# Tiles one by one, rows over two queues, blocks shared anew, and zero products in two waits

## The chip, the cores and the metric

The kernel runs on one core of a Trainium2 chip. The metric is the device time of one execution in microseconds, as the median of several runs. Five engines work side by side, each with an instruction stream of its own: TensorE (PE in the profile), VectorE (DVE), ScalarE (ACT), GpSimd (POOL) and SyncE (SP), which here only issues DMAs. GpSimd and ScalarE issue DMAs too, each on its own queue.

## The reference

The input x has 2048 tokens of 1024 features in bf16. Two layers are applied twice in turn, each on a normalised input and with a residual:

```python
x = A_x
x = x + _A_ref(_layernorm(x, axis=-1), A_w_r, A_w_i)
x = x + _B_ref(_layernorm(x, axis=-1), B_w1, B_b1, B_w2)
x = x + _A_ref(_layernorm(x, axis=-1), A_w_r, A_w_i)
x = x + _B_ref(_layernorm(x, axis=-1), B_w1, B_b1, B_w2)
```

`_A_ref` is a real two-dimensional Fourier transform over tokens and features, a product with the complex filter `w_r + 1j*w_i`, and the transform back, rounded to bf16. `_B_ref` is a dense layer to 3584 features, Mish (h times the hyperbolic tangent of its softplus), and a dense layer back to 1024.

```python
X = jnp.fft.rfft2(x.astype(jnp.float32), axes=(-2, -1)) * (w_r + 1j * w_i)
y = jnp.fft.irfft2(X, s=(S, D), axes=(-2, -1)).astype(jnp.bfloat16)
```

## The kernel before

**How it is written.** One program lists the instructions of each engine in order. `op`, `group` and `dma` add an instruction, a run of products, or a DMA, and work out its semaphore waits from resources (`Res`) that are read and written. So the order on each engine is the order of the Python calls, and an instruction that waits holds everything behind it on that engine. All DMAs have line 251. Large buffers lie in one tensor, ARENA, which is therefore the name most rows of a profile show; XS holds the 16 input tiles of 128 tokens, PS the eight banks of PSUM.

**The opening** (`prologue`, lines 382 to 413; `first_scales`, 582 to 604). x is loaded twice. First as 16 tiles of 128 tokens into XS, by seven DMAs of one to four tiles from SP and one from ScalarE (tile 10); for the mean and variance of each token VectorE handles tiles 0 to 9 (`stats_dve`, L472 and L475) and ScalarE tiles 10 to 15 (`stats_act`, L453). Then again as XR, in the arrangement that the Fourier transform needs, as 32 DMAs of 128 KB ("rows"): four quarters q of eight parts h. SP issues all of quarter 0 and the even parts of the others (20 rows), GpSimd the odd parts of quarters 1 to 3 (12 rows), after it has waited for tile 15. The table FD is loaded between quarters 2 and 3. After the rows SP issues the table JT, the first two filters `w_r`, `w_i` (four DMAs), the tables FT and BT, and small constants.

The statistics of all tiles are joined (L464 to L466), turned into one scale for each token (L444, L446), and transposed by TensorE (L596).

**Stage 1 of the first layer** (`s1`, lines 621 to 649; `scaled`, 606 to 619). The layer norm is folded into the matrix of the first Fourier step: the matrix M0 is multiplied by the scales of the tokens. That gives 16 scaled blocks, 0 to 15, in MN. Block 3 is made by ScalarE in eight instructions (L611), blocks 1, 4, 6, 8, 10, 12, 14 and 15 by GpSimd, the other seven by VectorE (L617). TensorE makes product j (eight matmuls, L636) from block j and quarter j // 4 of XR, into one of three pairs of banks. Its result is copied to Y by ScalarE (L642), or by VectorE (L644) where j leaves a rest of 1 when divided by 3. Blocks 0 to 3 are put on the engines first; block j + 4 comes after the copy of product j. Stage 2 (`s2`, L736) reads the whole of Y and FD; right after its first half come the products of the first filter (L994) and its copies on VectorE (L1005).

In the second layer's stage 1 there are no scaled blocks: XR comes from the normalised tokens, the last of them (tile 11) straight from SBUF in 16 small DMAs (`xr_direct`), in two halves. While they are under way TensorE makes 38 filler products (`spin(38, 7)`, line 1722, L653) whose result nobody reads.

**The end of a spectral layer** (`layer_A`, `residual_first`, and the first loop of `layer_B`, lines 1462 to 1466). The last of eight components (g = 7) is written to DRAM and read back in another arrangement, in four quarters. Meanwhile TensorE makes four filler products and puts the residual into all eight banks (`residual_first`, L1022). Then, for each quarter u, it adds the last transform step into banks 2u and 2u + 1 (`i4`, L1033), and ScalarE copies the banks out (`out_first`, L575). Statistics on VectorE follow, then transposes (L1143) and the first dense products (L1182).

Of the kernel before, what the change touches and what calls it, by code (L numbers as in the profile page):

```python
# [7 lines left out]
P = 128  # L8
# [172 lines left out]
class KB:  # L181
# [185 lines left out]
    def layout(self):  # L367
        K = 1024
        self.o = dict(XR=0, Z=0, X=12 * K, T=20 * K, YK=28 * K, V=40 * K, JT=48 * K, M0=49 * K, IDF=49 * K + 256, RT=50 * K,
                      JUNK=51 * K, WR=54 * K, YS=96 * K, UT=64 * K, MN=64 * K, Y=96 * K, XN=128 * K, U=128 * K,  # L370
# [11 lines left out]
    def prologue(self):  # L382
        sp = self.sp
        self.op(self.pool, lambda e: e.memset(self.EPS[:], 1e-5), writes=[self.r_eps, self.r_warm])
        xt = self.x[0].rearrange("(t p) d -> p t d", p=P)

        for a, b in ((10, 11), (0, 1), (1, 3), (11, 12), (3, 6), (12, 14), (6, 10), (14, 16)):
            self.dma(self.act if a == 10 else sp, self.XS[:, a:b, :], xt[:, a:b, :], f"x{a}", writes=self.r_xs[a:b])
        self.warm(ACT.Sqrt)
        small = {}  # L390
        def load_small(name, n, d):
            b = self.alloc(name, self.o[name], [n], d)
            self.dma(sp, b.ap, self.con[name], name.lower(), writes=[b.res])
            small[name] = b
        load_small("M0", P, BF)
        load_small("IDF", P, F32)
        self.M0, self.IDF = small["M0"], small["IDF"]

        self.XR = self.alloc("XR", self.o["XR"], [P, P])
        self.r_xr = []  # L400
        xv = self.x[0].rearrange("(n2 n1) (h l) -> h n2 n1 l", n2=16, l=P)
        for q in range(4):
            r = Res(f"xr{q}")
            for h in range(8):
                prog = self.pool if q and h % 2 else sp
                self.dma(prog, self.XR.ap[h:P:8, 32 * q:32 * q + 32, :], xv[h][:, 32 * q:32 * q + 32, :], f"xr{q}{prog.name}",
                         parts=[r], reads=[self.r_xs[15]] if prog is self.pool else [])
            self.r_xr.append(r)
            if q == 2:
                self.dma(sp, self.FD[:], self.con["FD"], "fd", writes=[self.r_fd])  # L410
        load_small("JT", 4 * P, BF)
        self.JT, self.r_jt = small["JT"].ap, small["JT"].res
        self.w1_next = 0
# [192 lines left out]
    def scaled(self, j):  # L606
        rt = self.RT
        rc = rt.ap.rearrange("p a b -> p (a b)")
        if j == 3:
            for n in range(8 * j, 8 * j + 8):  # L610
                self.op(self.act, lambda e, n=n: e.activation(self.MN.ap[:, n, :], self.M0.ap, ACT.Copy, scale=rc[:, n:n + 1]),  # L611
                        reads=[rt.res, self.M0.res], parts=[self.r_mn[j]])
            return

        n = slice(8 * j, 8 * j + 8)
        prog, sc, res = (self.pool, rc, rt.res) if j in (1, 4, 6, 8, 10, 12, 14, 15) else (self.dve, self.PS[:, 7, 0:P], self.r_bank[7])
        self.op(prog, lambda e: e.tensor_tensor(self.MN.ap[:, n, :], self.M0.ap.unsqueeze(1).to_broadcast([P, 8, P]),  # L617
                                                sc[:, n].unsqueeze(2).to_broadcast([P, 8, P]), ALU.mult),
                reads=[res, self.M0.res], parts=[self.r_mn[j]])

    def s1(self, li):
        self.Y = self.alloc("Y", self.o["Y"], [P, P])
        self.Y.res.begin()
        M, XR = self.M, self.XR
        for j in range(4 if not li else 0):
            self.scaled(j)
        for j in range(16):
            if not li and self.npair % 4 == 3:

                self.npair += 1  # L630
            ps, banks, _ = self.pair()
            fns = []
            for q in range(8):
                n = 8 * j + q
                m = M[:] if li else self.MN.ap[:, n, :]
                fns.append(lambda e, q=q, n=n, ps=ps, m=m: e.matmul(ps[:, q * P:(q + 1) * P], XR.ap[:, n, :], m,  # L636
                                                                   start=True, stop=True))
            self.group(fns, reads=[self.r_xr[j // 4], self.r_m if li else self.r_mn[j]], writes=banks)
            src = ps.rearrange("p (q k) -> p k q", q=8)
            dst = self.Y.ap[:, :, 8 * j:8 * j + 8]  # L640
            if (j % 2 or j == 8) if li else j % 3 != 1:
                self.op(self.act, lambda e, dst=dst, src=src: e.activation(dst, src, ACT.Copy), reads=banks, parts=[self.Y.res])  # L642
            else:
                self.op(self.dve, lambda e, dst=dst, src=src: e.tensor_copy(dst, src), reads=banks, parts=[self.Y.res])  # L644
            if not li and j + 4 < 16:
                self.scaled(j + 4)
        for r in ([self.MN.res, self.M0.res] + self.r_xr if not li else []):
            r.r(self.pe, self.pe.count)
            self.XR.res.r(self.pe, self.pe.count)

    def spin(self, n, bank):

        self.group([lambda e: e.matmul(self.PS[:, bank, :], self.BD[:, 0:P], self.BD[:, 0:512], start=True, stop=True)] * n,  # L653
                   reads=[self.r_bd], writes=[self.r_bank[bank]])

    def ring(self, name, n, size, shape):
        return [self.alloc(f"{name}{i}", self.o[name] + size * i, shape) for i in range(n)]
# [48 lines left out]
    def layer_A(self, li):  # L706
# [6 lines left out]
        o, K = self.o, 1024  # L713
        dve, act, sp, pool = self.dve, self.act, self.sp, self.pool
        ring, load_tabs, load_btabs, load_w = self.ring, self.load_tabs, self.load_btabs, self.load_w
        WT, FT, BT = self.WT, self.FTr, self.BTr
        FD, BD = self.FD, self.BD
# [7 lines left out]
        def zslot(g, i):  # L725
            return Z[(2 * g + i) % 6]

        def s2(g, half):
# [14 lines left out]
            else:  # L743
# [16 lines left out]

            zz = self.ARENA[:, o["Z"] // 2 + (2 * g % 6) * K:o["Z"] // 2 + (2 * g % 6 + 2) * K].rearrange(
                "p (s r k) -> p s r k", s=2, r=2)
# [157 lines left out]
        self.s1(li)  # L920
        if li:
            self.rest_of_filter()
        Z = ring("Z", 6, 2 * K, [2, 512])
        X = ring("X", 4, 2 * K, [2, 512])
        T = ring("T", 4, 2 * K, [2, 512])
# [32 lines left out]
                u_turn(g, h)  # L958
        self.spin(4, 0)
        self.residual_first()  # L960
        if li == 0:
            self.op(self.pool, lambda e: e.tensor_copy(self.B1[:], self.B1h[:]), reads=[self.r_b1h], writes=[self.r_b1])
        self.w1_buf = [self.alloc(f"W1_{i}", (self.ob["WS"] + i * 4096, 140 * K)[i > 4], [8, 256]) for i in range(4 if li else 6)]
# [155 lines left out]
    def layer_B(self, li, last):  # L1119
        pe, dve, act, sp, pool = self.pe, self.dve, self.act, self.sp, self.pool  # L1120
# [208 lines left out]
        def products(p, s_off, stages, extra, loads=True):  # L1329
# [14 lines left out]
            def s_sum(dst, x, y, op, k):  # L1344
                f = slice(7 * k, 7 * k + 7)
                self.op(dve, lambda e: e.tensor_tensor(ap[dst][:, f, :], ap[x][:, f, :], ap[y][:, f, :], op),  # L1346
                        reads=part(x, k) + part(y, k), writes=part(dst, k))
            s3, s1, s2, s4 = (lambda k, a=a: s_sum(*a, k) for a in (
                ("S", "A11", "A21", ALU.subtract), ("A21", "A21", "A22", ALU.add), ("A11", "A21", "A11", ALU.subtract),
                ("S", "A12", "A11", ALU.subtract)))  # L1350
# [53 lines left out]
            if stages is STD:  # L1404
                sums = {(0, 3): [(s1, 0)], (2, 0): [(s1, 1)], (2, 2): [(s2, 0)], (3, 0): [(s2, 1)], (3, 2): [(s4, 0)], (4, 1): [(s4, 1)]}
            else:
                sums = {(0, 1): [(s1, 0)], (0, 3): [(s1, 1)], (1, 1): [(s2, 0)], (1, 3): [(s2, 1)], (2, 3): [(s4, 0)], (3, 1): [(s4, 1)]}
# [53 lines left out]

        for u in range(4):
            self.i4(0, 4, 32 * u, 32, 2 * u)
            self.out_first(u, 0, act)
            for j in range(2):
                self.stats_quarter(j, u)
# [252 lines left out]
                self.xr_load(10)  # L1719
        products(1, self.ob["XT2"], stages, extra)  # L1720
        if not last:
            self.spin(38, 7)


def build_kernel(nc, A_x, A_w_r, A_w_i, B_x, B_w1, B_b1, B_w2, out):
# [35 lines left out]
```

## Time and profile before

| What | Value |
|---|---|
| Time, median of 3 runs | 933.21 us (932.65 to 934.0) |
| Time of the profiled execution | 934.83 us |
| Its span in the profile | 933.0 us |
| TensorE busy | 870.8 us, 93% of the span |
| VectorE, ScalarE, GpSimd busy | 620.8, 434.8, 158.9 us |
| Opening: first product of stage 1 / first of stage 2 | 24.23 / 40.60 us |
| First layer: last component written / first `i4` product | 106.81 / 116.17 us |
| Second layer: first filler product / first stage 1 product | 480.27 / 488.47 us |
| Second layer: last component written / first `i4` product | 558.67 / 566.33 us |

The profile is of one execution; times in it count from the start of the span. A name such as L636 is a line of the kernel. A busy TensorE is not one at its peak, as its matmuls are pipelined and their ends modelled. The idle time of an engine only matters where the chain of work that ended last passes through it.

The page's row on the granted TensorE clock, in 40 slices of 23.3 us, reads 9 (90% or more of full speed) in all but two slices, those from 117 us (8) and from 560 us (7).

### The profile page before, as it was taken

The page shows a single profiled execution, that of the slowest core. Times are in us where ns is not written, and L with a number is a line of the kernel's source. Part 1 is how long each engine was busy: PE and PEld are TensorE (multiplying, and loading weights), DVE is VectorE, ACT ScalarE, POOL GpSimd, SP SyncE. Part 2 cuts the span into 40 slices and gives each one's busy share as a digit, 9 for nine tenths or more (in the row PEclk, how much of TensorE's full clock was granted, in tenths as well). Part 3 has the DMA queues.
Part 4 walks back from the last instruction along what each step waited for, and adds up shares of the span by engine and source line. Part 5 has one row for each costly group of instructions (what it writes and reads, how often), then busy time and mean ns, then how long its engine had stood idle before and what let it go on. Part 6 is the DMA issues. An engine that isn't in the chain of part 4 may idle for free.

```text
span 933.0 us, 13477 instructions
## 1 busy us (share of the span) xinstructions
PE 870.8 (93%) x5404; PEld 470.5 (50%) x5479; DVE 620.8 (67%) x985; ACT 434.8 (47%) x641; POOL 158.9 (17%) x183
## 2 busy tenths in 40 slices
PE   0699689999999999999998987999999999999998
PEld 0577477444444444444447766764444444444443
DVE  6698367677698767558856865666747665554473
ACT  6798476455313385520009975847650015552000
POOL 3923002970003652010121200000000000000000
PEclk9999989999999999999999997999999999999999
DMA  9969862683886488364732795444166635732432
GB/s 277 256 232 294 220 162 67 223 301 102 294 246 222 154 301 321 132 207 156 275 103 79 236 224 145 159 152 165 57 192 191 198 126 194 278 119 76 175 123 111
DMA packets 147679, 175.99 MB, mean 189 GB/s; under 512 B 68872, under 2 KB 126312, under 8 KB 147496
## 3 DMA queue, kind: packets, MB, share of 16 engines
q1 hardware_dynamic: 134848, 128.81, 45.3%
q0 software_dynamic: 10672, 44.67, 13.2%
q10 hardware_dynamic: 2096, 1.64, 0.6%
q8 instruction: 43, 0.70, 0.3%
q14 instruction: 20, 0.16, 0.1%
HBM read 130.78 MB, written 40.89 MB: 184 GB/s over the span
## 4 chain that ended last, share of the span: by engine, by line
PE 84%; DVE 4%; ACT 4%; SPq 4%; DMA 3%; issue 1%; POOL 0%; ACTq 0%; DVEq 0%
PE PS L1321 36%; PE PS L1222 29%; PE PS L1182 6%; SPq L251 4%; PE PS L810 2%; PE PS L736 2%; PE PS L1033 2%; PE PS L835 2%; PE PS L1143 1%; DMA ARENA<-c_bt 1%; DMA ARENA<-u_scratch 1%; PE PS L653 1%; DMA u_scratch<-ARENA 1%; ACT ARENA L453 1%; DVE ARENA L792 1%
## 5 line engine op out<-in xcount | busy, mean ns | idle before, releaser
L1321 PE MATMUL PS<-ARENA 128*128 128x512 bf16 x1535 | 338.2, 379 | 1.7
L1222 PE MATMUL PS<-ARENA 128*128 128x512 f16 (+1 forms) x1265 | 279.0, 379 | 2.0 <-DVE ARENA L1227 0.8
L1321 PEld LDWEIGHTS PS<-ARENA 128*128 128x128 bf16 x1568 | 153.4, 98 | 184.4
L1227 DVE TENSOR_TENSOR ARENA<-PS,ARENA 128x512 f32<-128x512 f32 x230 | 157.1, 691 | 100.0 <-PE PS L1222 92.1
L1222 PEld LDWEIGHTS PS<-ARENA 128*128 128x128 bf16 x1288 | 125.4, 98 | 153.2 <-DVE ARENA L1227 3.5
L1232 ACT ACTIVATE ARENA<-ARENA,B 128x512 bf16<-128x512 f32 x138 | 98.8, 720 | 69.1 <-DVE ARENA L1227 63.7
L575 ACT ACTIVATE ARENA<-PS 128x512 f32<-128x512 f32 (+2 forms) x84 | 61.9, 742 | 115.1 <-PE PS L1222 92.3
L1115 POOL TENSOR_TENSOR ARENA<-ARENA 128x512 bf16<-128x512 bf16 x56 | 71.4, 1274 | 75.0 <-DVE ARENA L524 61.3
L453 ACT ACTIVATE ARENA<-XS 128x1024 bf16<-128x1024 bf16 x60 | 63.2, 1053 | 38.0 <-DVE XS L1372 33.1
L1182 PE MATMUL PS<-ARENA 128*128 128x256 bf16 (+1 forms) x524 | 74.1, 297 | 1.7 <-ACT ARENA L1186 1.4
L1346 DVE TENSOR_TENSOR ARENA<-ARENA 128x3584 bf16<-128x3584 bf16 x32 | 63.9, 2016 | 0.0
L1372 DVE TENSOR_TENSOR XS<-PS,ARENA 128x512 bf16<-128x512 f32 x52 | 35.7, 689 | 39.1 <-PE PS L1321 38.7
L1182 PEld LDWEIGHTS PS<-ARENA 128*128 128x128 bf16 x528 | 50.9, 99 | 20.5 <-ACT ARENA L1186 2.5
L1364 DVE TENSOR_TENSOR ARENA<-PS,ARENA 128x512 f32<-128x512 f32 x48 | 32.9, 688 | 28.1 <-PE PS L1321 27.7
L1186 ACT ACTIVATE ARENA<-PS,B 128x256 bf16<-128x256 f32 (+1 forms) x66 | 33.3, 516 | 29.6 <-PE PS L1182 29.3
L1232 ACT ACTIVATE ARENA<-PS,B 128x512 bf16<-128x512 f32 x46 | 31.5, 685 | 18.4 <-PE PS L1222 18.4
L1360 DVE TENSOR_TENSOR ARENA<-ARENA,XS 128x512 f32<-128x512 f32 x52 | 36.9, 734 | 0.6
L810 PE MATMUL PS<-ARENA 128*128 128x256 bf16 x256 | 32.4, 273 | 4.2 <-DVE ARENA L799 3.2
L444 ACT ACTIVATE RS<-MV,EPS 128x1 f32<-128x1 f32 (+2 forms) x11 | 3.3, 296 | 70.8 <-DVE MV L566 70.1
L788 ACT ACTIVATE ARENA<-PS 128x1024 bf16<-128x1024 f32 x32 | 33.3, 1071 | 4.5 <-PE PS L784 4.5
L792 DVE TENSOR_TENSOR ARENA<-ARENA 128x1024 bf16<-128x1024 bf16 x32 | 22.0, 688 | 19.5 <-ACT ARENA L788 13.8
L736 PE MATMUL PS<-FD,ARENA 128*128 128x256 bf16 (+1 forms) x256 | 31.8, 271 | 2.5 <-ACT ARENA L642 1.3
(97 smaller groups left out, 814.1 us busy)
## 6 DMA issues: line engine op xcount, KB each, us to landing
ARENA<-in_B_w_dram SPq DMA_DIRECT2D x30, 896.0 KB, 6.7
ARENA<-w1s_scratch SPq DMA_DIRECT2D x28, 896.0 KB, 4.6
ARENA<-w2s_scratch SPq DMA_DIRECT2D x24, 896.0 KB, 6.4
w1s_scratch<-ARENA POOLq DMA_DIRECT2D x14, 896.0 KB, 4.1
ARENA<-in_B_w_dram SPq DMA_DIRECT2D x24, 512.0 KB, 4.6
u_scratch<-ARENA SPq DMA_DIRECT2D x14, 512.0 KB, 3.5
ARENA<-u_scratch SPq DMA_DIRECT2D x14, 512.0 KB, 6.2
w2s_scratch<-ARENA POOLq DMA_DIRECT2D x8, 896.0 KB, 4.2
```

The source lines that it names most:

```text
L251: return eng.dma_start(out_ap, in_ap).then_inc(ds.sem, 16)
L453: self.op(act, lambda e, i=i, f=f: e.activation(junk.ap, x, f, accum_out=sums[:, i:i + 1]), reads=[self.r_xs[j]], writes=[junk.res], parts ...
L575: fn = (lambda e: e.activation(dst, src, ACT.Copy)) if scale is None else \
L736: fns.append(lambda e: e.matmul(dst, at(r), FD[:, t:t + n], start=start, stop=stop))
L810: fns.append(lambda e, c=c, part=part: e.matmul(ps[:, c * 256:(c + 1) * 256], yk.ap[:, part, c * P:(c + 1) * P], t[:, (128, 0)[part]:(384, ...
L1115: self.op(self.pool, lambda e, dst=A(dst), x=A(x), y=A(y), op=op: e.tensor_tensor(dst, x, y, op), reads=[b.res] + list(after), writes=[b.rs])
L1182: fns.append(lambda e, db=db, bank=bank, fl=fl: e.matmul(PS[:, bank, 0:w], wb.ap[:, db, fl * P:(fl + 1) * P], x.ap[:, db, tok], start=(db ...
L1222: self.group([lambda e, db=db: e.matmul(PS[:, bank, :], A[:, db, :], mov[:, db, :], start=(start and db == 0), stop=(db == 3), skip_group_ ...
L1227: self.op(dve, lambda e: e.tensor_tensor(dst.ap, PS[:, bank, :], x.ap, ALU.add), reads=[self.r_bank[bank], x.res], writes=[dst.res])
L1232: self.op(act, lambda e: e.activation(at, src, ACT.Mish, bias=self.B1[:, ft:ft + 1]), reads=[res, self.r_b1], writes=[ra])
L1321: self.group([lambda e, i=i, k=k, b=PB[n][k].ap: e.matmul(PS[:, bank, :], ap[:, i, t * P:(t + 1) * P], b[:, i - 7 * k, :], start=(start an ...
L1346: self.op(dve, lambda e: e.tensor_tensor(ap[dst][:, f, :], ap[x][:, f, :], ap[y][:, f, :], op), reads=part(x, k) + part(y, k), writes=part ...
```

## The change

It has five parts.

1. The tiles are loaded by 13 DMAs instead of 8: singly, but for 4 and 5, 6 and 7, 8 and 9. Tile 10 still comes from ScalarE.
2. GpSimd issues 19 of the 32 rows instead of 12: the odd parts of all quarters, and part 0 of quarters 1 to 3. It waits for tile 13 instead of 15. SP issues the other 13, and FD after all its rows instead of between quarters 2 and 3.
3. The scaled blocks: ScalarE makes block 1 instead of 3; GpSimd makes 2, 4, 9, 10, 11 and 13; VectorE the other nine. Of the copies of stage 1, VectorE keeps three (5, 10, 14) instead of five, and ScalarE has 13 instead of 11.
4. A new function, `hold`, makes n products of a weight matrix of zeros (ZERO, set by GpSimd after stage 1) with the constant table BD and adds them to bank 7. It is called after `residual_first`, with 16 products in the first layer and 11 in the second, and with two more between the first and the second quarter of `i4`.
5. The filler before the second layer has 33 products instead of 38.

```diff
-        for a, b in ((10, 11), (0, 1), (1, 3), (11, 12), (3, 6), (12, 14), (6, 10), (14, 16)):
+        for a, b in ((10, 11), (0, 1), (1, 2), (11, 12), (2, 3), (3, 4), (12, 13), (4, 6), (13, 14), (6, 8), (14, 15), (8, 10), (15, 16)):
             self.dma(self.act if a == 10 else sp, self.XS[:, a:b, :], xt[:, a:b, :], f"x{a}", writes=self.r_xs[a:b])
...
-                prog = self.pool if q and h % 2 else sp
+                prog = self.pool if h % 2 or q and not h else sp
                 self.dma(prog, self.XR.ap[h:P:8, 32 * q:32 * q + 32, :], xv[h][:, 32 * q:32 * q + 32, :], f"xr{q}{prog.name}",
-                         parts=[r], reads=[self.r_xs[15]] if prog is self.pool else [])
+                         parts=[r], reads=[self.r_xs[13]] if prog is self.pool else [])
             self.r_xr.append(r)
-            if q == 2:
-                self.dma(sp, self.FD[:], self.con["FD"], "fd", writes=[self.r_fd])
+        self.dma(sp, self.FD[:], self.con["FD"], "fd", writes=[self.r_fd])
...
-        if j == 3:
+        if j == 1:
             for n in range(8 * j, 8 * j + 8):
...
-        prog, sc, res = (self.pool, rc, rt.res) if j in (1, 4, 6, 8, 10, 12, 14, 15) else (self.dve, self.PS[:, 7, 0:P], self.r_bank[7])
+        prog, sc, res = (self.pool, rc, rt.res) if j in (2, 4, 9, 10, 11, 13) else (self.dve, self.PS[:, 7, 0:P], self.r_bank[7])
...
-            if (j % 2 or j == 8) if li else j % 3 != 1:
+            if (j % 2 or j == 8) if li else j not in (5, 10, 14):
...
+    def hold(self, n, bank):
+
+        self.group([lambda e: e.matmul(self.PS[:, bank, :], self.ZERO.ap, self.BD[:, 0:512], start=False, stop=False,
+                                       skip_group_check=True)] * n,
+                   reads=[self.r_bd, self.ZERO.res], writes=[self.r_bank[bank]])
...
         self.s1(li)
         if li:
             self.rest_of_filter()
+        self.ZERO = self.alloc("ZERO", o["RT"], [P])
+        self.op(pool, lambda e: e.memset(self.ZERO.ap, 0.0), writes=[self.ZERO.res])
...
         self.spin(4, 0)
         self.residual_first()
+        self.hold(11 if li else 16, 7)
...
         for u in range(4):
             self.i4(0, 4, 32 * u, 32, 2 * u)
+            if u == 0:
+                self.hold(2, 7)
             self.out_first(u, 0, act)
...
         if not last:
-            self.spin(38, 7)
+            self.spin(33, 7)
```

## The prediction

> **What bounds the kernel now.** I read the chain of work that ended last first, because it says where an earlier start is worth something, then the timeline of the opening, then the granted clock by stretches.
>
> ```profile
> PE 84%; DVE 4%; ACT 4%; SPq 4%; DMA 3%; issue 1%; POOL 0%; ACTq 0%; DVEq 0%
> ```
>
> TensorE ends the run for 84% of the span, and from 223 us to the end almost without a gap. What the change can touch lies in the other 16%: the opening (the first 41 us), the waits at the end of each spectral stage, and the filler products before the second one. Whatever they gain moves all later work, since the main loops follow in a fixed order.
>
> The opening, by the timeline (start, duration, engine, line; in brackets the wait and what ended it), first GpSimd's alone, then all engines:
>
> ```profile
> 16.11 7.61 POOL L251 DMA_DIRECT2D ARENA<-in_A_x_dram  x12 [15.25 <-DMA XS<-in_A_x_dram]
> 23.81 14.87 POOL L617 TENSOR_TENSOR ARENA<-ARENA 128x1024 bf16<-128x1024 bf16 x8
> ```
> ```profile
> 10.90 1.06 ACT L453 ACTIVATE ARENA<-XS 128x1024 bf16<-128x1024 bf16 x1 [1.40 <-DMA XS<-in_A_x_dram]
> ...
> 20.56 0.17 DVE L464 TENSOR_SCALAR MV<-BN 128x12 f32<-128x12 f32 x1 [1.03 <-ACT ARENA L453]
> ...
> 38.83 0.61 PE L636 MATMUL PS<-ARENA 128*128 128x128 bf16 x8 [0.58 <-POOL ARENA L617]
> ...
> 39.47 1.02 ACT L642 ACTIVATE ARENA<-PS 128x1024 bf16<-128x1024 f32 x1 [0.17 <-PE PS L636]
> ```
>
> The reader is to see three limits. ScalarE ends the statistics (VectorE waits 1.03 us for it), having lost 1.40 us to tiles 12 and 13, which come as one transfer. GpSimd sits until 16.11 for tile 15 before it issues its rows. And its eight scaled blocks end last: block 15 at 38.7 us, its product at 38.83, its copy at 40.49, then stage 2 at 40.60. In the same 15 to 18 us the DMA engines are a third idle (columns: stretch, length, busy of each engine, clock, DMA share, GB/s):
>
> ```profile
> 15.00:18.00 3.00, 0.00 (x0) 0.00 (x0) 2.90 (x8) 2.73 (x6) 1.89 (x3) 1.00 0.66 143
> 18.00:24.00 6.00, 0.48 (x1) 0.18 (x1) 3.82 (x12) 3.78 (x11) 5.90 (x11) 1.00 1.04 265
> ```
>
> The ends of the two spectral stages, in the same columns; first layer above, second below:
>
> ```profile
> 112.40:116.20 3.80, 0.03 (x2) 0.06 (x3) 0.00 (x0) 0.00 (x0) 0.00 (x0) 1.00 0.60 133
> 116.90:120.30 3.40, 2.81 (x106) 2.70 (x102) 2.26 (x6) 2.35 (x5) 0.00 (x0) 0.53 0.40 115
> ...
> 123.70:127.10 3.40, 3.40 (x31) 2.95 (x29) 3.26 (x7) 2.85 (x3) 0.00 (x0) 0.53 1.19 291
> ```
> ```profile
> 564.10:567.50 3.40, 1.05 (x33) 0.88 (x32) 0.00 (x0) 0.18 (x1) 0.00 (x0) 0.96 0.60 136
> 567.50:570.90 3.40, 2.65 (x96) 2.64 (x96) 1.60 (x5) 1.61 (x3) 0.00 (x0) 0.50 0.28 72
> 570.90:574.30 3.40, 1.55 (x21) 1.26 (x18) 3.20 (x10) 2.49 (x6) 0.00 (x0) 0.50 1.13 306
> 574.30:577.70 3.40, 3.40 (x35) 3.28 (x36) 2.57 (x5) 2.99 (x4) 0.00 (x0) 0.53 1.03 257
> ```
>
> TensorE stands idle while the last component goes to DRAM and back; then its clock is half for 6.8 us of the first layer and 10.2 of the second. The page's clock row dips in these two slices alone.
>
> **What the Trainium skill says.** "TensorE: Matmul & The Clock Gate", Part 1, says that the clock is gated to half after an idle window of about 3.4 us, that the window runs free of the kernel, and that a busy window releases it. The trace agrees: the half-clock stretches are multiples of 3.41 us, each after such a wait. It does not say whether products with zero weights count as activity; no line here shows it. "DMA: Bandwidth & Descriptors", Issuing engines are not separate DMA queues, says that more queues only save issue time; the 0.66 share shows a stretch where issue time is what lacks. "SBUF — State Buffer", SBUF size, gives GpSimd's descriptors 16 KiB of a partition; with 16 B each on 16 partitions ("DMA: Bandwidth & Descriptors", SWDGE vs HWDGE vs iDMA) an estimate is 16,384 places, against 19 rows x 512 pieces = 9,728, so a full ring is unlikely. No run here shows it.
>
> **The change, part by part.**
>
> *Tiles singly.* ScalarE has six tiles of about 2.37 us from 4.75, so 18.95 if it never waits, against 20.53. VectorE has ten of 1.40 from 4.57, so about 18.8 with small waits. Do tiles arrive? Two were there by 4.75, the eighth at 9.64 and the tenth at 10.90: 0.8 us a tile. In the new order ScalarE's tiles are the 4th, 7th, 10th, 13th and 16th, due 6.2, 8.6, 11.0, 13.5 and 15.9, and it needs them at 7.1, 9.5, 11.9, 14.2 and 16.6. So 1.55 us off the chain to the roots; blocks can start at 21.3 instead of 22.87. SP issues 12 instead of 7 at 0.52 us: its rows start at about 8.1, not 5.6, behind tiles that still fill the queue.
>
> *Rows.* GpSimd waits for tile 13 (the tenth, 11.0) and issues 19 rows at 0.634 us (7.61 / 12): free at 23.1, before 23.8. Queued behind this wait on GpSimd are its blocks. SP issues 13 rows instead of 20. The idle third of 15 to 18 us, 1.0 us of DMA time, fills, so rows, FD (now after the rows, first read at stage 2) and the filter loads come at least 1.0 us earlier. The last row landed at 35.9, FD takes about 2.5 us and lands by 35 us or so, under a stage 2 start at 37.
>
> *Blocks.* GpSimd has 6 x 1.86 = 11.2: ends 34.3, not 38.7. ScalarE makes block 1 (2.45) and 13 copies of 0.97: 21.45 + 2.45 + 12.6 = 36.5, plus 0.6 waiting for block 13's product: 37.1. VectorE makes 9 blocks of 1.17 and 3 copies of 1.22, 14.2 us, ending 36.7. This walk (each product waits for its block, its row quarter and a free pair of banks) gives 40.6 for the kernel before, measured 40.49. So stage 1 ends 3.4 us earlier, now bound by ScalarE. Late next is the first filter's load: it landed at 39.42, now at 38.4 if only the idle 1.0 us is gained; its product comes 0.87 us after stage 2 starts, at 38.0. It holds TensorE 0.4: I take **-3.0**. Bounds: -3.8 if the loads come 2.4 earlier, as fewer short pieces on SP's queue suggest, and the walk is a little cautious; -1.5 if only the statistics' gain comes through. The long wait at 70 to 80 us (BT's load, 9.5 us) is started by events that move along, so I carry the gain through.
>
> *Zero products, first layer.* 16 x 0.216 (the rate of the filler, L653) = 3.5 us in a wait of 3.8: they end 0.3 before the component lands. The memset is 0.1 us on an idle GpSimd. Two more between quarters cost 0.43 where the second quarter has landed, as here. Gain if the clock stays full: ahead of the first block of layer B the transposes take 1.42 (elsewhere 1.07), the fifteen small products 1.20 (0.64) and sixteen of L1182 2.48 (1.75), 1.6 on the chain, of which 1.4 follows after VectorE's copies. Net **-1.0**; bounds -1.5 and +0.8 (clock falls all the same, and the component comes early enough to be held up).
>
> *Second layer.* 11 x 0.216 = 2.4 in a wait of 2.1: 0.3 late, then 0.43, both under the second quarter, which lands at 568.2. Transposes 1.89 to 1.07, small products 1.20 to 0.64, L1182 1.90 to 1.75: 1.5. I take **-1.4**; bounds -1.7 and +0.3.
>
> *Filler 38 to 33.*
>
> ```profile
> 481.78 6.85 PE PS L653 x31
> 488.63 0.46 PE PS L636 x8
> ```
> ```profile
> ARENA<-ARENA SPq DMA_DIRECT2D x6, 16.0 KB, 2.4
> ```
>
> The chain runs through the filler (first fence), not through the rows. Of SP's six direct rows, issued from 483.34 on in 3.73 us, the third goes out at about 484.6 and takes 2.4 us (second fence: size and median time to landing): the first half lands near 487.0, and 33 products end at 487.55. The gain is 5 x 0.216 = 1.08; the second half, about 488.9, is needed after eight more groups. **-1.0**, bounds -1.1 and -0.3.
>
> Sum: -3.0 - 1.0 - 1.4 - 1.0 = **-6.4**. The profiled execution took 934.83 (span 933.0 and 1.8 around it), so it would be 928.4; it stood 1.6 above the median 933.21, so the median is **926.8**.
>
> **Rivals.**
> 1. *The clock falls all the same* (zero weights don't count, or the later gaps of 1.7 us are enough, as after 120.3). For it: the second half-speed stretch of the first layer follows a window with 1.57 us busy. Against: at 77 to 80 us TensorE is idle 3 us with a full clock after. Then -3.0 - 1.0 + 0.4 = -3.6: 929.6.
> 2. *The opening's gain is eaten by loads.* Tables and filters queue behind the same rows; stage 2 starts early and waits. For it: the chain of before passes through the filter's load (34.42, 4.99 us). Then -0.8 - 2.4 - 1.0 = -4.2: 929.0.
> 3. *Slower: GpSimd's issue.* Block 2 is now the third product and lies behind 19 issues. For it: the longest single issue in the trace is 1.09 us; 19 such end at 31.7, block 13 at 42.9, its copy and that of block 15 at about 45.6, 5.1 later than now. With the other -3.4 that is +1.7: 934.9. It decides from about 1.0 us an issue, where the opening loses 3.4. Against: twelve in a row took 0.634 each under the same statistics.
>
> **How the numbers follow.** Forecast 0.60 (own range 924.8 to 929.0), clock 0.17, loads 0.10, GpSimd 0.09, anything else 0.04. The range 924.8 to 931.8 takes in the first three with their bounds and leaves out the slower case and the tails. A difference of 0.2% is 1.9 us, about what a measurement of this kernel can tell from no change. Faster beyond it: 0.83; within: 0.08; slower: 0.09.
>
> **What would show it.** GpSimd's first row at about 11 us and its first block at 23; L464 at 19; stage 2 (L736) at 37 to 38; clock 1.00 in the 10 us after each component; the filler ending at the same distance before L636. A first block on GpSimd past 27 us, L736 after 40, or half clock after the zero products would show a step wrong; so would TensorE waiting for rows after 33 filler products.

## The result, and the profile after

The changed kernel takes 933.63 us (median of 6 runs, 932.72 to 934.68), the kernel before in the same comparison 933.43 (6 runs, 932.39 to 934.0). The ratio is 1.0004 with an interval of 0.9991 to 1.0017: no change that can be measured, where 926.8 was forecast. The profiled execution took 934.68 us with a span of 932.9 (before 934.83 and 933.0).

Following one point of each stage through the two profiles splits the forecast sum into what came of each term. A minus is earlier; each row is the change within its own stretch. The component goes to DRAM in two writes; "written" is the start of the first. In the views of the changed kernel a line has its number there: L635 is L636 of the kernel before, L1041 its L1033, L1190 its L1182.

| Term | Forecast, us | Profile, us | Read from (before, after) |
|---|---|---|---|
| Opening, carried to the last component | -3.0 | 0.0 | stage 2 at 40.60, 40.90; component written at 106.81, 106.81 |
| End of the first layer | -1.0 | +0.41 | 17th product of L1190 (before: L1182) at 128.51, 128.92 |
| Filler 38 to 33 | -1.0 | -1.07 | stage 1 of layer 2 at 488.63, 487.97, so -0.66, of which +0.41 was there before |
| End of the second layer | -1.4 | +0.50 | 17th product of L1190 at 579.67, 579.51 |
| Sum | -6.4 | -0.16 | span 933.0, 932.9 |

**The opening.** GpSimd does what was forecast. In the timeline of the changed kernel (start, duration, engine, line; in brackets the wait and what ended it) its rows begin at 10.51 us, one every 0.63 us, and its blocks at 22.55. The instruction that joins the statistics (L464 before, L463 here) begins at 19.19, against 20.56:

```profile
10.51 11.94 POOL L251 DMA_DIRECT2D ARENA<-in_A_x_dram  x19 [9.65 <-DMA XS<-in_A_x_dram]
22.55 11.16 POOL L616 TENSOR_TENSOR ARENA<-ARENA 128x1024 bf16<-128x1024 bf16 x6
```

TensorE, in the same view, makes products 0 to 3 early (8 + 24 matmuls) and then stands still:

```profile
24.12 2.74 PE L635 MATMUL PS<-ARENA 128*128 128x128 bf16 x24 [0.25 <-ACT ARENA L610]
29.45 8.03 PE L635 MATMUL PS<-ARENA 128*128 128x128 bf16 x80 [2.59 <-issue]
37.98 0.62 PE L635 MATMUL PS<-ARENA 128*128 128x128 bf16 x8 [0.51 <-DVE ARENA L616]
39.12 0.62 PE L635 MATMUL PS<-ARENA 128*128 128x128 bf16 x8 [0.51 <-DVE ARENA L616]
40.90 1.03 PE L741 MATMUL PS<-FD,ARENA 128*128 128x256 bf16 x8 [1.16 <-DVE ARENA L643]
```

Product 4 is the first that needs quarter 1 of the rows. The profile puts its 2.59 us down to "issue", that is, to nothing that it shows; the semaphore events in the trace name the row: the last one of quarter 1 on SyncE's queue, issued at 15.20 us, signals its landing at 29.36. GpSimd's rows of that quarter were all there by 22.82. The rest of the stage then runs late into VectorE, which the chain of waits shows (start, length, what): the copy of product 10, then blocks 14 and 15 queued behind it, then the last copy.

```profile
26.86 2.59 issue
29.45 6.10 PE PS L635 x56
35.55 0.02 issue
35.58 1.23 DVE ARENA L643
36.80 2.26 DVE ARENA L616 x2
39.06 1.15 DVE ARENA L643
```

The pause has a second cost. The 56 matmuls behind it take 6.10 us, 0.109 each; in the run with early quarters below, 24 take 1.51, 0.063 each. This slow stretch ends at 35.36 us, where the trace has its first record of the granted clock; before it the views print 1.00 without a record.

Why the row was late is in the DMA view of 24 to 28 us (the packets of all queues; then each queue's packets, MB and share of 16 engines), and in the view of SyncE's own DMAs from 18 to 34 us (duration of one issue, then issue to landing: least, median, most):

```profile
DMA packets 643, 0.93 MB, mean 232 GB/s; under 512 B 437, under 2 KB 437, under 8 KB 643
...
q0 software_dynamic: 305, 0.84, 91.6%
q1 hardware_dynamic: 338, 0.08, 14.3%
```
```profile
L251 SPq DMA_DIRECT2D ARENA<-in_A_x_dram x6: 630/1834/4734, 15.9 to 28.8; - x6
...
DMA to landing us min/median/max: 3.3/7.2/13.6
```

q0 is GpSimd's queue, q1 that of SyncE. 206 packets are over 2 KB (643 less 437) and carry the 0.84 MB: 4096 bytes each. SyncE's have 256 bytes (0.08 MB in 338). In these 4 us SyncE's queue moved a tenth of what GpSimd's did. Over the longer stretch its issues took from 0.63 us to as much as 4.73, and one row took 13.6 us to land. The rows of GpSimd's queue that landed in the 4 us are of quarters 2 and 3, which nothing needed yet.

**The ends of the spectral stages.** The zero products run where they were meant to, and the clock is full through the wait. It falls one window later (stretch, length, busy of TensorE, weight loads, VectorE, ScalarE, GpSimd, then clock, DMA share, GB/s); the first layer first, then the second:

```profile
117.53:120.94 3.41, 2.59 (x97) 2.45 (x95) 2.41 (x7) 2.37 (x5) 0.00 (x0) 1.00 0.79 222
120.94:124.35 3.41, 1.82 (x31) 1.67 (x32) 3.05 (x9) 3.19 (x6) 0.00 (x0) 0.96 1.19 295
124.35:127.76 3.41, 3.41 (x30) 2.83 (x28) 3.38 (x7) 2.84 (x4) 0.00 (x0) 0.54 1.15 279
```
```profile
568.10:571.50 3.40, 2.00 (x81) 1.90 (x77) 2.24 (x8) 2.55 (x5) 0.00 (x0) 0.96 0.66 187
571.50:574.90 3.40, 2.95 (x30) 2.75 (x31) 2.65 (x7) 2.60 (x5) 0.00 (x0) 0.50 1.20 290
574.90:578.30 3.40, 3.40 (x29) 2.85 (x28) 3.21 (x7) 2.76 (x4) 0.00 (x0) 0.53 0.60 144
```

Before, the first layer had two half-clock stretches of 3.4 us; now it has one, the second of them. The second layer has 6.8 us instead of 10.2. The trace's records of the clock put the two falls at 124.11 and 571.25, so each lies about a quarter of a microsecond before the end of a stretch shown here. The timeline of the first layer:

```profile
112.14 3.66 PE L657 MATMUL PS<-BD,ARENA 128*128 128x512 bf16 x16
116.34 0.95 PE L1041 MATMUL PS<-MT,ARENA 128*128 128x32 bf16 x32 [0.54 <-DMA ARENA<-u_scratch]
117.35 0.38 PE L657 MATMUL PS<-BD,ARENA 128*128 128x512 bf16 x1
117.57 2.55 PE L1041 MATMUL PS<-MT,ARENA 128*128 128x32 bf16 x96
121.78 0.81 PE L1041 MATMUL PS<-MT,ARENA 128*128 128x96 bf16 x15 [1.67 <-ACT XS L574]
123.34 1.24 PE L1151 MATMUL PS<-IDENT,ARENA 128*128 128x128 bf16 x16 [0.75 <-DVE ARENA L523]
```

After `i4` TensorE waits 1.67 us for ScalarE to copy out, and 0.75 us for VectorE before the transposes. The second pause and most of the first lie in the 3.41 us before the fall, 120.70 to 124.11, of which TensorE is busy 1.58.

**The filler** works as forecast: 6 + 26 recorded products, then stage 1 at once, on the chain, with no wait for rows.

```profile
480.85 1.29 PE PS L652 x6
482.14 0.05 issue
482.19 5.78 PE PS L652 x26
487.97 0.46 PE PS L635 x8
```

### The profile page after: what moved, and what is told of

The parts are those of the page before. It is cut to its first block, busy times and chain, and to the rows that moved or that the text cites. A ratio compares the mean times of both kernels' runs of the same rounds, so it can differ in the third digit from the quotient of the medians.

```text
span 932.9 us, 13539 instructions
## 1 busy us (share of the span) xinstructions
PE 878.9 (94%) x5428; PEld 476.0 (51%) x5505; DVE 619.2 (66%) x985; ACT 436.9 (47%) x643; POOL 160.0 (17%) x190
## 4 chain that ended last, share of the span: by engine, by line
PE 85%; ACT 5%; DVE 5%; DMA 3%; issue 1%; POOL 0%; SPq 0%; ACTq 0%; DVEq 0%
PE PS L1329 36%; PE PS L1230 29%; PE PS L1190 6%; ACT ARENA L452 2%; PE PS L815 2%; PE PS L741 2%; PE PS L1041 2%; PE PS L840 2%; PE PS L635 1%; PE PS L1151 1%; DMA ARENA<-c_bt 1%; DMA ARENA<-u_scratch 1%; DMA u_scratch<-ARENA 1%; PE PS L652 1%; DVE ARENA L797 1%
## 5 line engine op out<-in xcount | busy, mean ns | idle before, releaser
L1190 PE MATMUL PS<-ARENA 128*128 128x256 bf16 (+1 forms) x524 | 75.1, 300 | 1.7 <-ACT ARENA L1194 1.4
L1190 PEld LDWEIGHTS PS<-ARENA 128*128 128x128 bf16 x528 | 51.4, 100 | 21.0 <-ACT ARENA L1194 2.5
```

Of the source, the lines that this page charges most:

```text
L1190: fns.append(lambda e, db=db, bank=bank, fl=fl: e.matmul(PS[:, bank, 0:w], wb.ap[:, db, fl * P:(fl + 1) * P], x.ap[:, db, tok], start=(db ...
```

## The experiments

Two things had to be explained: why quarter 1 came late, and why the zero products gave nothing. All edits are against the changed kernel unless said otherwise. The kernel before was run beside each set, with medians of 932.53, 933.05 and 932.24 us, so ratios are compared rather than times. The time of one execution varies by several microseconds (the kernel before: 930.48 to 935.22 in 46 runs).

### The rows as before

```diff
-                prog = self.pool if h % 2 or q and not h else sp
+                prog = self.pool if q and h % 2 else sp
...
-                         parts=[r], reads=[self.r_xs[13]] if prog is self.pool else [])
+                         parts=[r], reads=[self.r_xs[15]] if prog is self.pool else [])
             self.r_xr.append(r)
-        self.dma(sp, self.FD[:], self.con["FD"], "fd", writes=[self.r_fd])
+            if q == 2:
+                self.dma(sp, self.FD[:], self.con["FD"], "fd", writes=[self.r_fd])
```

> The changed kernel with the rows as before: GpSimd 12 of 32 after tile 15, SP 20, FD between quarters 2 and 3. Theory (GpSimd's rows go ahead of SP's on the DMA engines, so a row of quarter 1 on SP came only when GpSimd's 19 were through): quarter 1 lands at about 27.0 and quarter 3 at 35.8 as in the kernel before, product 4 of stage 1 starts near 27 instead of 29.45, and stage 2 begins at 39.5 to 40.0 instead of 40.90. Rival (quarter 1 is late because tiles and constants of SP come first, whoever issues the rows): product 4 stays at 29 or later and stage 2 at 40.5 or later.

932.17 us, ratio 0.9995 (0.9984 to 1.0006). In its profile product 4 starts at 28.9 us and stage 2 at 40.6. So undoing the rows brings the opening back by 0.3 us only, close to the rival's side; the 27 us of the theory did not come. With 12 rows on GpSimd's queue and 20 on its own, SyncE's part of quarter 1 is there at 28.9, hardly earlier than with 19 and 13: the old division isn't the one that the earlier statistics and new blocks need.

### GpSimd takes the quarters needed first

```diff
-                prog = self.pool if h % 2 or q and not h else sp
+                prog = self.pool if q < 2 else sp
```

> The changed kernel with all 16 rows of quarters 0 and 1 on GpSimd and all of quarters 2 and 3 on SP. Theory (GpSimd's queue goes ahead): quarters 0 and 1 land by 19 and 24, SP's after that at 0.65 us a row, by 29 and 33; TensorE never waits for rows, stage 2 begins at 37.5 to 38.5, 2.5 to 3.4 us earlier than in the changed kernel. If what follows keeps it, the time is 0.25 to 0.35 percent lower; if the wait for BT's table to 79.97 takes it (it ended at the same 79.97 in both kernels although stage 2 began 0.3 apart), the last component is still written at 106.8 and the time doesn't change. Rival (the DMA engines share evenly and the total decides): quarter 1 lands at 27 or later and stage 2 begins after 40.

931.5 us, ratio 0.999 (0.9982 to 0.9998). The timeline of TensorE:

```profile
27.39 1.51 PE L635 MATMUL PS<-ARENA 128*128 128x128 bf16 x24 [0.83 <-DMA ARENA<-in_A_x_dram]
...
33.18 1.51 PE L635 MATMUL PS<-ARENA 128*128 128x128 bf16 x24 [0.69 <-DMA ARENA<-in_A_x_dram]
...
36.93 1.03 PE L741 MATMUL PS<-FD,ARENA 128*128 128x256 bf16 x8 [1.16 <-DVE ARENA L643]
38.98 0.63 PE L1002 MATMUL PS<-ARENA 128*128 128x256 bf16 x4 [1.01 <-DMA ARENA<-in_A_w_i_dram]
```

Product 4 starts at 27.39 and stage 2 at 36.93, 3.97 us before that of the changed kernel and inside the 37 to 38 of the forecast, but for 0.07. So the blocks and copies were walked rightly, and the landing of quarter 1 was what spoiled it. The filter's load now holds TensorE 1.01 us, the "late next" of the forecast. The wait for the table BT moves along (9.29 us, from 67.39), and the last component is written at 103.65, 3.16 earlier than in the changed kernel. The kernel was run again in the last set:

> The kernel of e2_gpsimd_early_quarters once more, as the partner on the same chip of the two kernels without zero products: early rows, 16 + 2 and 11 + 2 zero products, no fill. 930.5 to 932.

932.01 us, ratio 0.9998 (0.9982 to 1.0014). Stage 2 at 37.30, but the last component only at 105.42, 1.4 earlier than in the changed kernel. In this execution the filter's load held TensorE 1.11 us, and the granted clock was at half from 39.58 to 42.99. It is the exception: in the other 13 profiles of this document, the kernel before among them, the component is written 65.8 to 67.1 us after the start of stage 2, here 68.1. So a start gained in the opening is carried through, as the forecast had it, if the clock isn't lost right behind it. In the medians this edit alone is worth about 1 us, not told apart from nothing.

### No row on GpSimd at all

```diff
-                prog = self.pool if h % 2 or q and not h else sp
+                prog = sp
```

> All 32 rows on SyncE's queue, none on GpSimd's. If GpSimd's packets of 4096 bytes hold up SyncE's of 256, SyncE's rows now come at an even pace: the 16 rows of quarters 0 and 1 are there by 26 us, no row takes more than 9 us from its issue to its landing, and SyncE has no single issue over 2.5 us after the tiles. If SyncE's queue is slow of itself in this stretch (its own issuing, or the table loads beside it), quarter 1 is not there before 28 us, and issues of 3 us and more stay. In both cases the last quarter is later than in the changed kernel, 33 us or more, so the time is no better.

A single run took 934.38 us. The DMA view of 24 to 28 us and SyncE's own DMAs from 18 to 34 us, as shown above for the changed kernel:

```profile
DMA packets 3158, 0.79 MB, mean 198 GB/s; under 512 B 3157, under 2 KB 3157, under 8 KB 3157
...
q1 hardware_dynamic: 3157, 0.78, 86.8%
```
```profile
L251 SPq DMA_DIRECT2D ARENA<-in_A_x_dram x22: 627/628/636, 17.8 to 31.9; - x22
...
DMA to landing us min/median/max: 2.8/3.1/5.3
```

With GpSimd's queue empty, SyncE issues a row every 0.63 us without one exception, and a row lands 3.1 us after its issue. The same queue moved 0.78 MB in these 4 us, against 0.08. TensorE's timeline then has product 4 in one run with products 1 to 3, and pays at quarter 3, whose last row has 31 in front of it:

```profile
23.92 5.62 PE L635 MATMUL PS<-ARENA 128*128 128x128 bf16 x56 [0.25 <-ACT ARENA L610]
...
36.23 3.29 PE L635 MATMUL PS<-ARENA 128*128 128x128 bf16 x32 [3.57 <-DMA ARENA<-in_A_x_dram]
40.68 1.03 PE L741 MATMUL PS<-FD,ARENA 128*128 128x256 bf16 x8 [1.16 <-DVE ARENA L643]
```

For quarter 1 this settles where the cause lies: neither the issuing nor the bandwidth of SyncE's queue is short; it is GpSimd's queue beside it. In the changed kernel both queues together moved more (232 against 198 GB/s), but rows that were not needed first.

### The changed kernel once more

> The changed kernel itself once more, on the chip that the next kernels use. If the landing of SyncE's rows is decided anew in every execution, product 4 of stage 1 starts at another time than 29.5 us (between 26 and 31 us), and stage 2 moves with it (36.7 to 41.5), while the GpSimd queue's last row lands at 29 to 32 us as before. If the order of the instructions decides it, product 4 starts within 0.5 us of 29.5. Time against the kernel before: 0.998 to 1.001 in both cases.

934.31 us, ratio 1.0009 (0.9993 to 1.0025), 12 runs from 929.19 to 936.8. Product 4 at 29.12, stage 2 at 39.85. Two further kernels below have the same code in the opening, and there product 4 starts at 27.94 and 26.57, stage 2 at 38.76 and 36.75. The repeat alone would have spoken for a landing fixed by the order of the instructions, being within 0.4 of 29.45. With the other two it is decided anew in each execution, 26.57 to 29.45 in four profiles, and the opening that was forecast does occur, with the same code, in one of the four. The share of SyncE's queue goes with it: in the same 4 us it moved 0.21, 0.14, 0.13 and 0.08 MB where product 4 starts at 26.57, 27.94, 29.12 and 29.45.

### The zero products left out

```diff
-        self.hold(11 if li else 16, 7)
...
-            if u == 0:
-                self.hold(2, 7)
```

> The changed kernel without any zero products (16 and 2 in the first layer, 11 and 2 in the second). Theory (they keep the clock through the wait itself, but a window of 3.4 us with two short pauses right after it drops it all the same, and the two between the quarters cost 0.4 in the first layer): the clock falls in the first layer just after the component lands, and again from about 124; the second half of the first layer's end is 0.4 earlier relative to the component's landing; the time is within 0.1 percent of the changed kernel. Rival (the zero products gain what was forecast, hidden by another loss): 1.5 to 2.5 us slower than the changed kernel.

931.78 us, ratio 0.9983 (0.9969 to 0.9997), against 1.0004 (0.9991 to 1.0017) and 1.0009 (0.9993 to 1.0025) with them: faster without them by about 0.2%, which neither side of the expectation had; the intervals just overlap. Half clock at 114.5 to 121.3 and 565.0 to 571.9. To have the openings alike, the same edit was made to the kernel with the early quarters:

> The same with all zero products left out, so that the difference is theirs alone. The forecast had them at a gain of 2.0 (1.0 + 1.4 less 0.4 for the two more): then this is 2 us slower than its partner, 933. If they cost time, as the two profiles with and without them suggest (the component has landed before they end, and the clock falls after them all the same), it is 1 to 2 us faster, 929.5 to 930.5.

930.12 us (20 runs, 928.86 to 931.86), ratio 0.9976 (0.9968 to 0.9984), against 0.9998 for its partner and 0.999 for the same kernel in the first set: the zero products cost 1.3 to 2 us, where they were forecast to gain 2.4. The profiles show why they gain little: the clock falls all the same. They don't show the cost: from the write of the last component to the 17th product of L1190 they explain 0.6 us in the first layer and 0.5 in the second, and of the 2.4 us between the two spans (931.1 and 928.7) 1.6 are there when the component is written, before any zero product. Nor is it the clock: over all executions its mean is 0.995 to 0.996 with the zero products and 0.992 without them, so half clock became shorter and the time longer. What costs the rest stays open.

### The pauses after `i4` filled

```diff
         self.root(0, 2)
+        self.spin(3, 0)
         rest(0)
+        self.spin(3, 4)
```

> The changed kernel with three filler products before the first small products of the transform's rest and three more before the transposes, in free banks, so that the pauses of 1.7 and 0.7 us after the last component are shorter. Theory (the window with those pauses is what drops the clock): the clock stays full from the component to the dense layer in both layers, transposes 1.07 instead of 1.24 to 1.89 and sixteen L1182 products 1.75 instead of 2.66, 1.0 to 1.5 us for each layer, so 0.1 to 0.3 percent faster than the changed kernel. Rival (zero weights count as idle, so the wait before is what drops it): half clock as in the changed kernel, no gain.

932.31 us, ratio 0.9993 (0.9978 to 1.0009), runs from 927.93 to 936.23. Its profile, of an execution of 927.93, has full clock from the opening to 925.5 us, and the transposes take 1.08 us, the sixteen products of L1190 1.92 with nothing at half rate. The clock is measured in every execution, not only in the profiled one: its mean is 1.000 in 5 of these 12 and in none of the 18 of the changed kernel. So filling the two pauses can keep the clock, though not each time. What it is worth in time isn't resolved here, within a spread of 8 us.

### Early quarters, fill, and the number of zero products

The three edits together, with 16 and 11, with 9 and 6, with none, and with 9 and 11 zero products after `residual_first`:

```diff
-        self.hold(11 if li else 16, 7)
+        self.hold(11 if li else 9, 7)
```

> GpSimd takes all of quarters 0 and 1, SyncE quarters 2 and 3, and the pauses of the second layer's end are filled with products of no use (3 and 4 of them). If the two repairs are independent: stage 2 starts at 36.5 to 37.5 us, the clock is full from the last component to the end, and the time is 926 to 928.5, 0.993 to 0.996 of the kernel before. If the early start is given back at the last component (table BT), or the fill only moves the throttling elsewhere, it is 930 or more.

> As the kernel before it in this list, with 9 zero products instead of 16 in the first layer's wait and 6 instead of 11 in the second's. If the zero products often end after the component has landed (16 last 3.7 us, and i4 begins 7.7 us after the write at the earliest, where 6.25 us were seen without them), this gains up to 1 us more: 925 to 928. If the shorter run of products lets the clock fall before i4, it loses 1 to 2 us against it.

> Early rows and the products of no use in the pauses before the transposes, but no zero products. If the fill keeps the clock only together with the zero products, the clock falls at the first i4 of each layer and this is no faster than without the fill, 929.5 to 930.5. If the fill does it alone, 927.5 to 929.

> Early rows, fill, 9 zero products in the first layer and 11 in the second (with 6 there the clock fell at 562.4 us, with 11 it didn't). If the 6 lost what the throttle took (6.8 us at half clock, 1 to 2 us) it is faster than the kernel with 9 and 6 (0.9964): 0.994 to 0.996 of the kernel before. If the 11 end after the component has landed, that is given back, and it is 0.996 to 0.998.

| Early quarters, and | us | Ratio (interval) | Half clock at the two ends in the profile, us | Executions with a mean clock of 1.000 |
|---|---|---|---|---|
| 16 and 11, no fill | 932.01 | 0.9998 (0.9982 to 1.0014) | 3.4 and 3.4 | 0 of 12 |
| none, no fill | 930.12 | 0.9976 (0.9968 to 0.9984) | 10.2 and 6.8 | 0 of 20 |
| none, fill | 930.04 | 0.9977 (0.9965 to 0.9989) | 3.4 and 3.4 | 0 of 10 |
| 16 and 11, fill | 930.17 | 0.998 (0.9969 to 0.999) | 0 and 0 | 12 of 20 |
| 9 and 6, fill | 929.35 | 0.9964 (0.9954 to 0.9974) | 0 and 6.8 | 7 of 20 |
| 9 and 11, fill | 928.85 | 0.9961 (0.995 to 0.9973) | 0 and 0 | 6 of 11 |

The kernel with 16 and 11 missed the 926 to 928.5 that two independent repairs would give: its clock was full, but in its profile stage 2 began at 38.57 instead of 36.5 to 37.5, the filter's load held TensorE 1.4 us at 39.6, and the component was written at 105.69. The one with 9 and 6 missed its range by 1.35 us and lost the clock in the second layer, as its expectation had for too short a run. The one without zero products came out as expected where the fill needs them: half clock at the first `i4`, and no gain from the fill (930.04 against 930.12). Zero products alone lose 1.3 to 2 us, fill alone gives nothing, and only with both did an execution keep the full clock throughout, in about half of the cases. Within each of the three kernels that have both, the executions with a mean clock of 1.000 have a median 1.7 to 1.9 us below that of the others; this is what was seen, not what an edit brought about. The kernel with 9 and 6 took 0.8 us less than that with 16 and 11 on the same chip, but their intervals overlap, so the number of zero products is not shown to matter. The last kernel lies on the border of its two ranges. Its timeline in stretches of 3.41 us, with the two pauses, now filled, in the second line:

```profile
110.53:113.94 3.41, 3.29 (x104) 2.64 (x103) 0.83 (x3) 1.19 (x2) 0.00 (x0) 1.00 0.34 75
113.94:117.35 3.41, 2.23 (x54) 1.78 (x51) 3.25 (x10) 2.86 (x6) 0.00 (x0) 1.00 0.84 240
117.35:120.76 3.41, 3.12 (x44) 2.35 (x41) 3.12 (x7) 3.26 (x4) 0.00 (x0) 1.00 1.19 295
```

The clock stays full. Busy time alone does not decide that, though. In the changed kernel's second layer it fell after 3.41 us with 2.26 busy (567.84 to 571.25), more than the 2.23 here. And in the kernel with no row on GpSimd, which has 16 zero products and no fill, it stayed full in the first layer after 3.41 us with 1.76 busy (120.98 to 124.39) and both pauses. Of the twelve layer ends that were profiled with 16 or 11 zero products and no fill, this is the only one that kept the clock. The timeline of the last kernel shows the zero products end just as the component lands:

```profile
108.61 2.15 PE L657 MATMUL PS<-BD,ARENA 128*128 128x512 bf16 x9
110.88 0.95 PE L1041 MATMUL PS<-MT,ARENA 128*128 128x32 bf16 x32
...
115.98 0.82 PE L652 MATMUL PS<-BD 128*128 128x512 bf16 x3 [1.18 <-ACT XS L574]
```

That is 6.5 us after the second, last write of the component. With 16 products `i4` began 7.85 to 9.22 us after it in all eight profiles; with 9, at 6.50 and 6.53; with none, at 6.25, 6.61 and 8.36, and in the kernel before at 8.29. In the changed kernel the 16 end 7.92 us after the write, so they would hold a component that lands at 6.3 back by 1.6 us. In seven of the eight the component landed after their end, though; whether they delay the landing itself was not tried.

The kernel with 9 and 11 has the lowest median of all: 928.85 us, 0.9961 of the kernel before, and faster than the changed kernel too by the two ratios. It is not told apart from the one with 9 and 6, nor clearly from the one that has neither zero products nor fill (930.12), since the intervals overlap.

## Why the prediction was wrong

**Statistics and tiles: right.** 19.19 for the 19 that was to be looked for (L463 here, L464 before), 1.37 us earlier for the 1.55 of the forecast, ScalarE without its wait of 1.40.

**GpSimd's issue: right.** 0.628 us a row (11.94 / 19), first block at 22.55. The slower rival, stretched issues on GpSimd, did not happen. The stretch fell on SyncE. Nor did a full ring show, which the forecast had called unlikely: the 19 issues took 0.63 to 0.79 us each. (The 16 bytes of a descriptor that its estimate uses stand in the section Terms of the page it names.)

**Rows: the step that failed.** The forecast had it that the idle third "fills, so rows, FD (now after the rows, first read at stage 2) and the filter loads come at least 1.0 us earlier". That holds for the last row, which the trace has at 32.1, against 35.9, for FD at 34.4 and for the first filter, at 38.4 as forecast. It does not hold for quarter 1, the one that product 4 needs, at 29.36. The walk gave every quarter the gain of the mean. The rest of that part holds: with the same opening in the run with fill, product 4 starts at 26.57 and stage 2 at 36.75. The Trainium skill, "DMA: Bandwidth & Descriptors", Queues, rings and completion order, has what might have warned: each engine takes turns between queues packet by packet. The forecast drew on the same page only for issue time and for the room for descriptors. The trace agrees in direction: with packets of 4096 bytes beside 256, SyncE's queue moved a tenth of what GpSimd's did (0.08 and 0.84 MB); strict turns would give a sixteenth, an estimate from the two sizes. But in the kernel before, with the same sizes and in the same 4 us, SyncE's queue moved 0.33 MB beside 0.62. So the sizes alone don't set the share, and no run here separates them from another advantage of GpSimd's queue. The rival "opening's gain is eaten by loads" had -0.8 left of it; what took it were rows, not tables.

**Zero products: the second step that failed.** "Gain if the clock stays full" had a condition, and it fell. Zero weights do count: the half-clock stretch from 116.7 is gone. But the forecast took each half-clock stretch to follow the long wait ("each after such a wait"). The one from 123.5 did not: the 3.41 us ahead of it (120.10 to 123.51, busy 1.39) already held the two pauses behind `i4`, which zero products in the wait don't touch. The first rival had named them. With the zero products the clock still falls there, and with the pauses filled it can stay full. So in the first layer the part behind `i4` takes 8.80 us before and after. What is left is +0.41 ahead of it: `i4` begins 0.17 later and takes 0.24 longer with the two extra products, which were put at 0.43. In the second layer the part behind `i4` takes 9.41 instead of 8.68, since the half clock now lies over the products of L1190 (2.82 us for sixteen, 2.10 before); 0.23 of this was made up ahead of it. The skill, "TensorE: Matmul & The Clock Gate", HAM oscillation — how this bites in real kernels, gives the rule of no idle gap over about 3.4 us. Here no gap was longer than 1.67, and the clock fell: the measurement decides. The first rival's 929.6 kept a full opening, so it was right on the clock and wrong on the sum.

**Filler: right.** -1.07 for -1.0.

**The sum.** -6.4 became -0.16: 3.0 lost with the rows, and 3.3 with the clock (+0.9 instead of -2.4). A gain of one microsecond in the filler is what remained to set against the cost of the zero products.

## What to carry to other kernels

When DMAs that a kernel needs in order are spread over a GpSimd queue and another one, look at the bytes that each moves in the critical stretch, and put what is needed first on the one that gets more, here GpSimd's. Then ask for each landing time by itself, not for a mean gain. To keep TensorE's clock, cover the short pauses behind the long wait too: zero products in the wait alone cost 1.3 to 2 us here, and with both the clock was full in about half of the executions of the three kernels above. And the number of filler products in a wait is worth a run of its own, since the landing behind it varied by 2 us here.

## What was not expected of the hardware

- Two queues can carry more together (232 against 198 GB/s) while one of them moves 0.08 MB in 4 us instead of 0.78.
- SyncE's issues are held up with it: up to 4.73 us for one, 0.63 with the other queue empty.
- The same opening in four profiles of three kernels had product 4 at 26.57, 27.94, 29.12 and 29.45 us: the outcome of the two queues differs between executions, and the bytes that SyncE's queue moved from 24 to 28 us fall in the same order, 0.21, 0.14, 0.13 and 0.08 MB.
- Products with zero weights keep the clock up: it is full from 112.14 to 120.94 us, through a wait behind which it was half before.
- Short pauses can cost the clock: it fell with no gap longer than 1.67 us. No share of busy time separates the cases: it fell after 3.41 us with 2.26 busy and stayed full after 3.41 us with 1.76 busy.
- With the same kernel the clock is full in some executions and not in others (12 of 20, 7 of 20 and 6 of 11 in the three kernels with both fillings).
